# Cosine attention with a token and channel mixer: pair 0 loaded by heads, the end of batch 0 reordered, q and k loaded five pairs ahead

## The chip, the cores and the metric

The kernel runs on one core of a Trainium2 chip. The metric is the device time of one execution in microseconds (us); lower is better. Engines are named as the profile names them: PE is TensorE (matmuls), PEld its weight loads, DVE is VectorE, ACT is ScalarE, POOL is GpSimd, SP is SyncE, which issues most transfers. "Pair" means two heads of one batch; there are 8 batches of 6 pairs, so pairs 0 to 47. The kernel before takes 386.36 us (median of the first three runs).

## The reference, cut to what matters

```python
q_n = q / (norm(q) + 1e-6);  k_n = k / (norm(k) + 1e-6)      # (8, 12, 448, 64)
attn = softmax(q_n @ k_n.T / tau)                              # tau = 0.1
x = (attn @ v) as (8, 448, 768)
u = x + (relu(x.T @ w_tok1) @ w_tok2).T                        # token mixing, 448 -> 256 -> 448
out = u + relu(u @ w_ch1) @ w_ch2                              # channel mixing, 768 -> 1536 -> 768
```

## The kernel before

A pair goes through this: load q and k; square them (GpSimd or ScalarE); sum the squares (VectorE, `sums`); logarithm and exponential on ScalarE, then a small sum and a reciprocal on VectorE (`norms`); multiply by the reciprocal norm on GpSimd (`scale`); transpose (PE) and copy out (VectorE); score (PE) and exponential (ScalarE); output (PE) and division (VectorE); token mixing. Once the six pairs of a batch are through, channel matmuls of that batch fill PE. In the first batch there is none of that filler yet, so there every engine's order counts. In the orders in time of these traces POOL, VectorE and ScalarE do their instructions in the order in which they are recorded: POOL, for one, stands 0.96 us before the copy of w2n at 18.63 us, with pair 3's scale behind it. The source reads:

```python
def norms(i, a0=0, a1=2, dve=False):           # a: 0 is k, 1 is q
    ...
    if dve:
        nc.vector.tensor_reduce(out=rn, in_=ne, ...)
        nc.vector.reciprocal(out=rn, in_=rn)
        return
    nc.scalar.activation(out=rn, in_=st["ssq"][0:n, sl], func=AF.Ln, bias=tiny[0:n])
    nc.scalar.activation(out=ne[:, :, 0], in_=rn, func=AF.Exp, scale=0.5)

def scale(i, a, eng=None):
    eng = eng or nc.gpsimd
    ...
    eng.tensor_tensor(out=kq[...], in0=st["kq"][a][...], in1=_bcast_free(rn[...], E), op=ALU.mult)
# ... cut: square, sums, tpose, score, pv_wide, tok1, tok2, udma (a transposing DMA), m_ch1

with tc.manual_schedule():
    # ... cut: loads, pair 0's squares, norms and scales
    sums(1); norms(1)
    tpose(0, 1, 2); warm(3, True); tpose(0, 0, 1); warm(5, True)
    square(2, 0)
    weights_tok2()                             # POOL issues the load of w2n
    score(0, 0); score(0, 1)
    norms(1, dve=True)
    scale(1, 0); scale(1, 1, nc.vector)
    sums(2); norms(2)                          # pair 2's norms: between pair 0's scores
    cast_v(0)
    score(0, 2); warm(8); tpose(1); score(0, 3); warm(6)
    norms(2, dve=True)
    square(3, 1, act=True); square(3, 0)
    load_v(4); load_qk(6)

    for i in range(1, NPAIR):                  # NPAIR = 6
        if i == 1:
            scale(2, 0); scale(2, 1, nc.vector)     # q of pair 2 on VectorE
        else:
            scaled(i + 1)                           # k and q on GpSimd
            if i != 3:
                weights_ch1(max(i - 3, 0))          # 576 KB, issued by POOL
        load_qk(i + 6)
        score(i, 0); score(i, 1)
        sums(i + 2); norms(i + 2)
        if i >= 2:
            tok1(i - 2)
        pv_wide(i - 1)
        norms(i + 2, dve=True)
        cast_v(i); square(i + 3, 0)
        # ... cut
        if i == 1:
            place_w2()                              # POOL copies w2n into w2t
        # ... cut
    # ... cut: pair 6; then pair 7, where batch 0 ends:
        if i == NPAIR + 1:
            tok2(i - 2, pe=True); upose(i - 4, 2); upose(i - 2)
            sums(i + 2)
        pv_rest(i - 1); pv(i - 1, 0); pv(i - 1, 1)
```

## Time and profile before

| stretch (us) | what happens | what was full |
|---|---|---|
| 0 to 15 | loads, pair 0, no filler for PE | a chain over all engines |
| 15 to 38 | pairs 1 to 6, one per 4.18 us | ACT and POOL |
| 38 to 46 | the end of batch 0 | POOL; PE idle 1.26 of 7.54 us |
| 46 to 352 | pairs with channel matmuls between | PE |
| 352 to 385 | last channel matmuls | PE |

A row of the table by stretch gives the stretch, its length, then for each engine the busy time and in brackets the instructions, then the granted clock of PE (1.00 is full), the mean DMA share, and GB/s. The prediction below shows these rows. A row of the order in time gives the start, the duration, the engine, the source line, the operation and its tiles, and in square brackets how long the engine was idle before it and what ended that. First the table's row for the 14 us that follow batch 0, with its header:

```profile
core 0: us, PE busy (x) PEld busy (x) DVE busy (x) ACT busy (x) POOL busy (x), PEclk, DMA share, GB/s
46.00:60.00 14.00, 14.00 (x172) 8.84 (x173) 8.79 (x21) 11.34 (x19) 11.15 (x14) 1.00 1.17 240
```

PE doesn't idle there at all. And from ScalarE's order in time, its wait for the sums of pair 9's squares:

```profile
44.46 0.31 ACT L264 ACTIVATE rn<-ssq,tiny 112x16 f32<-112x16 f32 x1 [1.18 <-DVE ssq L253]
```

### The profile page before, as it was taken

To read this page: it belongs to the slowest core of one execution; us is meant where nothing else is said; L and a number is where in the kernel's file an instruction comes from. 1 tells how busy PE (TensorE), PEld (TensorE's weight loads), DVE (VectorE), ACT (ScalarE), POOL (GpSimd) and SP (SyncE) were. 2 spreads that over 40 slices of the span, in tenths; PEclk is the share of its full clock that TensorE was granted. 3 is DMA by queue.
4 is the path that set the end of the run, shared out by engine and by line. 5 is a ranking of instruction groups with operands and counts; after the bars stand their busy time and mean duration, and the time that the engine had idled before them with its cause. 6 is when DMAs were issued, how large, how long until landed. Compare 5 with 4: busy or idle time off the path is not lost.

```text
span 385.4 us, 10226 instructions
## 1 busy us (share of the span) xinstructions
PE 372.2 (97%) x4124; PEld 243.3 (63%) x4124; DVE 217.4 (56%) x520; ACT 226.6 (59%) x398; POOL 237.8 (62%) x383
## 2 busy tenths in 40 slices
PE   5989899999999999999999999999999999999995
PEld 4566566677656666667666666667666666665564
DVE  7789766777535674557545674566544674241032
ACT  5899687845665456855675466764675466601400
POOL 8799987979567667668557767768657733000000
PEclk9799999999999999999999999999999999999998
DMA  8999999995984888768894887977996745114023
GB/s 214 263 244 235 157 235 190 226 222 112 243 191 116 200 204 201 175 168 177 213 195 117 172 204 185 197 173 181 198 217 122 134 120 133 15 54 97 0 67 99
DMA packets 115423, 64.21 MB, mean 167 GB/s; under 512 B 71728, under 2 KB 111792, under 8 KB 115376
## 3 DMA queue, kind: packets, MB, share of 16 engines
q1 hardware_dynamic: 108944, 57.62, 68.2%
q0 software_dynamic: 5616, 5.21, 8.9%
q10 hardware_dynamic: 816, 0.73, 0.7%
q8 instruction: 32, 0.52, 0.6%
q14 instruction: 15, 0.12, 0.1%
HBM read 43.45 MB, written 11.01 MB: 141 GB/s over the span
## 4 chain that ended last, share of the span: by engine, by line
PE 87%; DMA 4%; ACT 4%; DVE 2%; POOL 1%; issue 1%; ACTq 0%; DVEq 0%; POOLq 0%
PE psF L449 28%; PE psG L433 28%; PE psO L362 9%; PE psS L323 7%; PE psU L407 5%; PE psR L393 5%; DMA ut<-u 3%; ACT pt L324 3%; PE psQ L330 2%; PE psO L345 1%; DMA qf<-in_q_dram 1%; PE pst L300 1%; ACT sq L235 1%; POOL sq L237 1%; DVE ssq L253 0%
## 5 line engine op out<-in xcount | busy, mean ns | idle before, releaser
L324 ACT ACTIVATE pt<-psS 128x896 f16<-128x896 f32 (+1 forms) x156 | 132.6, 916 | 58.2 <-PE psS L323 57.8
L433 PE MATMUL psG<-ut,wc1t 128*128 128x448 f16 x576 | 116.8, 352 | 0.5 <-DMA ut<-u 0.5
L449 PE MATMUL psF<-wc2t,gt 128*128 128x384 f16 (+2 forms) x684 | 116.2, 323 | 0.0
L436 ACT ACTIVATE gt<-psG 128x448 f16<-128x448 f32 x96 | 51.8, 540 | 63.0 <-PE psG L433 63.0
L276 POOL TENSOR_TENSOR kq<-kf,rn 128x384 f16<-128x384 f32 (+1 forms) x48 | 42.8, 892 | 73.6 <-DVE rn L262 70.3
L449 PEld LDWEIGHTS <-gt 128*128 128x128 f16 x684 | 64.2, 98 | 38.0
L433 PEld LDWEIGHTS <-wc1t 128*128 128x128 f16 x576 | 53.8, 98 | 44.9 <-issue 0.7
L453 DVE TENSOR_TENSOR ost<-psF,u 128x384 f32<-128x384 f32 (+2 forms) x65 | 34.5, 531 | 57.1 <-PE psF L449 56.9
L253 DVE TENSOR_REDUCE ssq<-sq 128x15 f32<-128x960 f32 (+2 forms) x49 | 55.8, 1140 | 4.2 <-ACT sq L235 3.6
L396 DVE TENSOR_SCALAR rt<-psR 128x256 f16<-128x256 f32 x48 | 20.1, 419 | 59.5 <-PE psR L393 59.4
L276 POOL TENSOR_TENSOR kq<-qf,rn 112x512 f16<-112x512 f32 x45 | 46.9, 1043 | 3.0
L323 PE MATMUL psS<-qk 64*128 64x448 f16 x312 | 41.7, 359 | 2.7 <-DVE qk L302 2.5
L237 POOL TENSOR_TENSOR sq<-kf 128x384 f32<-128x384 f32 (+1 forms) x46 | 40.1, 872 | 1.2 <-DMA kf<-in_k_dram 1.2
L362 PE MATMUL psO<-vt,pt 128*128 128x65 f16 (+1 forms) x1056 | 40.3, 193 | 0.2 <-DVE ut L424 0.2
L237 POOL TENSOR_TENSOR sq<-qf 112x512 f32<-112x512 f32 x39 | 40.5, 1039 | 0.0
L362 PEld LDWEIGHTS <-pt 128*128 128x128 f16 (+1 forms) x1056 | 35.2, 97 | 4.0 <-PE psS L323 1.0
L366 DVE TENSOR_TENSOR x<-psO,rec 128x256 f16<-128x256 f32 x84 | 35.6, 424 | 2.9
L410 DVE TENSOR_TENSOR u<-psU,x 128x512 f16<-128x512 f32 x48 | 32.3, 674 | 4.8 <-PE psU L407 3.6
L393 PEld LDWEIGHTS <-w1t 128*128 128x128 f16 x384 | 25.0, 98 | 9.0 <-issue 2.3
L407 PEld LDWEIGHTS <-w2t 128*128 128x128 f16 x384 | 24.9, 98 | 7.8 <-issue 1.5
L393 PE MATMUL psR<-x,w1t 128*128 128x128 f16 x384 | 29.3, 219 | 0.4 <-DVE u L410 0.3
L407 PE MATMUL psU<-rt,w2t 128*128 128x128 f16 x384 | 29.3, 219 | 0.2 <-DVE qk L302 0.2
(54 smaller groups left out, 282.8 us busy)
## 6 DMA issues: line engine op xcount, KB each, us to landing
qf<-in_q_dram SPq DMA_DIRECT2D x48, 224.0 KB, 4.2
kf<-in_k_dram SPq DMA_DIRECT2D x36, 192.0 KB, 3.4
vf<-in_v_dram SPq DMA_DIRECT2D x36, 192.0 KB, 3.7
vf<-in_v_dram SPq DMA_DIRECT2D x12, 224.0 KB, 7.3
out_dram<-ost SPq DMA_DIRECT2D x8, 336.0 KB, 3.6
wc1t<-in_moe_w_ch_dram POOLq DMA_DIRECT2D x4, 576.0 KB, 10.2
wc2t<-in_moe_w_ch_dram POOLq DMA_DIRECT2D x2, 1152.0 KB, 14.0
out_dram<-ost SPq DMA_DIRECT2D x8, 288.0 KB, 3.3
```

The costliest lines, as they stand in the source:

```text
L237: nc.gpsimd.tensor_mul(out=dst, in0=src, in1=src)
L253: nc.vector.tensor_reduce(out=st["ssq"][0:n, sl], in_=st["sq"][0:n, sl], axis=AXX.X, op=ALU.add)
L276: eng.tensor_tensor(out=kq[0:p, a, 0:n].rearrange("p c g e -> p g c e"), in0=st["kq"[a]][:].rearrange("p (g c) e -> p g c e", g=2), in1=_b ...
L323: nc.tensor.matmul(psS[:, hh, 0:S], qk[hb, c * n:c * n + 128], qm[hb], start=True, stop=True)
L324: nc.scalar.activation(out=pts[i % 2][0:n, 2 * S * c:2 * S * (c + 1)].rearrange("p (h s) -> p h s", h=2), in_=psS[0:n, :, 0:S], func=AF.Ex ...
L362: nc.tensor.matmul(psO[:, m, 0:E + 1], pts[i % 2][0:n, at:at + 128], vt[0:n, i % HP, nch * hh + c, 0:E + 1], start=(old(i) and c == 0), st ...
L366: nc.vector.tensor_tensor(out=st["x"][:, :, hh * E:(hh + 1) * E], in0=psO[:, :, 0:E], in1=_bcast_free(rec[:], E), op=ALU.mult)
L393: nc.tensor.matmul(psR[:, tt], w1t[:, w1[m], tt * 128:(tt + 1) * 128], st["x"][:, m], start=(m == 0), stop=(m == 3))
L407: nc.tensor.matmul(psU[:, m], w2t[:, tt, lo:lo + 128], st["rt"][:, tt], start=(tt == 0), stop=(tt == TT - 1))
L433: nc.tensor.matmul(psG[:, 0:S], wc1t[:, dt, ct * 128:(ct + 1) * 128], ut[b][:, dt].rearrange("p m s -> p (m s)")[:, lo:lo + S], start=(dt ...
L436: nc.scalar.activation(out=gt[:, ct, (b % 2) * S:(b % 2 + 1) * S], in_=psG[:, 0:S], func=AF.Relu)
L449: nc.tensor.matmul(psF[:, 0:hi - lo], gt[:, ct, at:at + 128], wc2t[:, ct, lo:hi], start=(ct == 0), stop=(ct == CT - 1))
```

## The change

It has three parts. **The prologue**: pair 0's q and k come in by heads on two queues, k of pair 0 is scaled and transposed in halves, and pair 1's norms and scales come earlier; to make room, pair 2's norms and both of its scales move behind pair 1's first exponential. **The end of batch 0**: PE's work is recorded in the order in which VectorE can serve it, and pair 6's output goes into a tile of two banks. **Loads**: from pair 3 on, q and k are loaded five pairs ahead instead of six.

```diff
+    def load_first(a, src):                      # q or k of pair 0, one head per queue
+        t = qkv.tile([SC, QS, E], FP32, ...)
+        for g, eng in ((0, nc.sync), (1, nc.scalar)):
+            eng.dma_start(out=t[:, NCH * g:NCH * (g + 1)]..., in_=src[0, g]...)
+        return t
-            (nc.scalar if nm == "k" and i < 3 else nc.sync).dma_start(
+            nc.sync.dma_start(
... cut: scale_part (scale of chunks c0 to c1), tpose with chunks, x_wide split from pv_wide
-        for dt in range(DT):
+        dts = (0, 1, 3, 4, 2, 5) if (b, ct) == (0, 0) else range(DT)
... prologue
-        scale(0, 0)
+        scale_part(0, 0, 0, 2, nc.gpsimd)
+        scale_part(0, 0, 2, NCH, nc.gpsimd)
...
-        sums(2)
-        norms(2)
         cast_v(0)
         score(0, 2)
...
-        norms(2, dve=True)
+        sums(2)
...
         for i in range(1, NPAIR):
-            if i == 1:
-                scale(2, 0)
-                scale(2, 1, nc.vector)
-            else:
+            if i > 1:
                 scaled(i + 1)
...
-            load_qk(i + 6)
+            if i != 3:
+                load_qk(i + (6 if i < 3 else 5))
             score(i, 0)
+            if i == 1:
+                norms(2)
+                norms(2, dve=True)
+                scaled(2)
             score(i, 1)
... the end of batch 0, at pair 7
             if i == NPAIR + 1:
+                upose(i - 4, 2)
                 tok2(i - 2, pe=True)
-                upose(i - 4, 2)
+                pv_wide(i - 1)
                 upose(i - 2)
+                x_wide(i - 1)
                 sums(i + 2)
-            pv_rest(i - 1)
-            pv(i - 1, 0)
-            pv(i - 1, 1)
+            else:
+                pv_rest(i - 1); pv(i - 1, 0); pv(i - 1, 1)
```

The same move of `load_qk` from six to five ahead is made for pair 6 and for all later pairs.

## The prediction

> **What bounds the kernel now.** I read first the page's busy shares, then a table of busy time by stretch, then the order of instructions in time for the first 46 us, and last the chain of work that ended last. The share of busy time alone says that TensorE (PE) is the bound; the table says where it isn't.
>
> ```profile
> PE 372.2 (97%) x4124; PEld 243.3 (63%) x4124; DVE 217.4 (56%) x520; ACT 226.6 (59%) x398; POOL 237.8 (62%) x383
> ...
> core 0: us, PE busy (x) PEld busy (x) DVE busy (x) ACT busy (x) POOL busy (x), PEclk, DMA share, GB/s
> ...
> 8.00:14.60 6.60, 5.49 (x41) 3.23 (x39) 5.06 (x11) 4.65 (x9) 5.39 (x7) 0.50 1.20 254
> 15.00:38.00 23.00, 20.29 (x360) 14.66 (x357) 19.81 (x42) 22.84 (x39) 22.04 (x25) 1.00 1.16 246
> 38.37:45.91 7.54, 6.28 (x90) 4.19 (x88) 6.49 (x16) 4.76 (x8) 7.54 (x9) 1.00 1.29 126
> 45.91:352.00 306.09, 305.75 (x3410) 199.97 (x3410) 173.68 (x423) 182.60 (x321) 195.40 (x319) 1.00 0.80 170
> ```
>
> From 45.91 to 352 us PE is busy 305.75 of 306.09 us, and the change leaves that work alone (as it does the last 33 us, a tail of matmuls). So only the first 46 us can pay. In them PE is not the bound: from 15 to 38 us ScalarE (ACT) is busy 22.84 of 23 us and GpSimd (POOL) 22.04, and the DMA engines carry about 250 GB/s throughout. Each pair of heads there takes 4.18 us (the first softmax exponential of pairs 1 to 6 starts at 15.38, 19.56, 23.74, 27.93, 32.11 and 36.30). From 8 to 14.6 us PE has half its clock (0.50). Between 38.37 and 45.91 no engine but POOL is full: that is the end of batch 0, a chain between PE and VectorE (DVE).
>
> ```profile
> 10.59 0.81 POOL L182 DMA_DIRECT2D w2n<-in_moe_w_tok_dram  x1 [0.64 <-DMA w1t<-in_moe_w_tok_dram]
> 11.41 1.06 POOL L276 TENSOR_TENSOR kq<-kf,rn 112x512 f16<-112x512 f32 x1
> ...
> 14.57 1.55 POOL L276 TENSOR_TENSOR kq<-kf,rn 112x512 f16<-112x512 f32 x1 [0.56 <-DVE rn L262]
> ...
> 18.63 0.99 POOL L185 COPY w2t<-w2n 128x896 f16<-128x896 f16 x1 [0.96 <-DMA w2n<-in_moe_w_tok_dram]
> 19.59 1.04 POOL L276 TENSOR_TENSOR kq<-kf,rn 112x512 f16<-112x512 f32 x1
> ...
> 32.01 13.02 DMA ut<-u
> 45.02 0.04 issue
> 45.07 0.92 PE psG L433 x4
> ```
>
> The first rows are POOL's own order: its first scale of pair 1's k stands behind an issue that waited for an earlier weight load, and from 18.63 us on POOL never stops until pair 7 is scaled at 38.23. The last three are the chain: the transposing DMA of pair 2's output, issued at 32.01, lands 13.02 us later, and the channel matmul that needs it starts then, at 45.07.
>
> **What the Trainium skill says.** "TensorE: Matmul & The Clock Gate", Part 1, says that the array runs at half clock after an idle window and gets the full one after about 3.4 us of sustained work. The trace agrees: PE did 0.82 us of work between 5 and 8 us, then had 0.50 until 14.6. "DMA: Bandwidth & Descriptors", Anatomy of one DMA, fits a DMA from GpSimd as 2.0 us plus bytes over 436 GB/s: 2.5 us for the 224 KB of w2n. The list of DMA issues has 8.0 us for it; with the engines saturated the formula doesn't hold, and I use 8.0. "VectorE: DVE Perf Modes", the TRN2 errata section, gives a float32 tensor_tensor as (N+151)/0.96 ns: 691 for 512 elements, 424 for 256. The trace has 691 and 425. So a product over both heads in one instruction costs 0.69 us where two cost 0.85; with the reciprocals (0.20 against 2 x 0.17) it saves 0.30 us of DVE.
>
> **The change part by part.**
>
> *Pair 0's load by heads.* q of pair 0 goes out in two halves on two queues, then k. Now q and k share the engines, and q lands at 4.27 us, k at 4.72. Their 448 KB move at some 270 to 350 GB/s, so q alone should land about 0.7 us sooner, k hardly. VectorE's norms of pair 0 end at 7.83 now; with k's square waiting for k I get 7.2. POOL is issuing the eight w1t loads until 7.42, so its scale of k starts at 7.45 rather than 7.92.
>
> *k in halves.* A scale of 1.04 us becomes two of about 0.55. The first half is transposed, copied out and scored while the second runs. First score at about 8.75 instead of 10.06. ACT, however, has pair 1's norms ahead of it in order, which need pair 1's squares summed (about 9.35 by my count), so the first exponential starts near 9.9 instead of 10.65: 0.7 us won.
>
> *What then waits.* The w2n issue still stands ahead of pair 1's k on POOL, and still needs w1t to have landed (10.3 us). So that scale starts at 11.1 to 11.4 as before, the fourth score of pair 0 follows it at about 13, and pair 1's first exponential comes at 13.9 to 15.0 against 15.38: 0.4 to 1.5 us won.
>
> *Pair 2.* Its norms move behind pair 1's first exponential, and both of its scales go to POOL (before, q was on DVE, 0.69 us). From that exponential: 0.86 for it, 0.53 for logarithm and exponential, 0.5 on DVE, then on POOL 2.04 (two scales), 0.6 (cast), 1.0 (square) and 1.0 (placing w2n): POOL reaches pair 3's scale 6.5 us after it, at 20.4 to 21.5 instead of 19.59. That is a loss of 0.8 to 1.9 us on POOL. Its 18.64 us of unbroken work for pairs 3 to 7 passes that on to pair 7. I choose 0.9. Unless w1t lands early, the prologue's gain is eaten here.
>
> *End of batch 0.* Between 38.37 and 45.91 PE has, at its pace in the chain: transposes 0.40, token matmuls 3 x 0.45 (one psR, two psU), pair 7's scores 0.67, transposes of outputs 0.60, pair 6's output 1.13, channel matmuls 1.14. Sum 5.29 of 7.54 us, so at most 2.25 us is waiting. The new order follows DVE: outputs of pair 4 are done before the transposes, the psO tile in the other pool takes no slot that DVE must free first, and pair 2's transposed block, late in landing, is used fifth of six instead of third (two matmuls, 0.38 us, of grace). Counted from POOL's end for pair 7: 1.25 us to the scores, then 0.67, 0.40, 0.65 (with a wait for rt), 1.13, 0.40 and 1.25, in all 5.75 us. With POOL 0.9 late, at 39.13, the first channel group ends at 44.9 against 45.98 now: 1.1 us won.
>
> *Loads five pairs ahead.* No bytes are saved. Pair 9's q and k (448 KB, about 1.8 us at 250 GB/s) no longer stand ahead of pair 2's transposing DMA, and pair 10's move behind it too, so it should land at 41.5 to 44, before its matmul needs it. The price: k of pairs 10 and 11 lands later (I get 45 and 52 where they landed at 39.0 and 49.8), and POOL already waited 1.2 us for k of pair 11. Some of this reaches PE through DVE's sums: I take 0.3 us of loss.
>
> Sum: 1.1 - 0.3 = 0.8 us by the count. A change of this kind to a tuned kernel is probably kept for a reason, and my count of POOL is the weakest part, so I choose 1.4 us.
>
> **The rivals.** (1) *POOL takes the place of ACT.* For it: the order above, and 22.04 busy of 23 us. At its worst, POOL 1.9 us late, it leaves 0.1 us of gain, and with loads late the kernel would be slightly slower, about 387. Against it: if w1t lands sooner because ACT's queue empties early, pair 1's scale starts a microsecond earlier, nothing is lost on POOL, and the gain is 2 us, with the clock regained earlier 2.5 to 3: about 383.5. (2) *The transposing DMA stays the wait.* It lands late where it runs beside the w1-channel weight load, and that load is still there. If it lands at 45.0 again, two matmuls follow instead of four: 0.4 us won, about 386. (3) *Late loads.* If POOL waits 3 us for pair 11 and the sums of that pair hold DVE, the gain goes in waits of PE between 50 and 60 us: about 386.3. (4) *Everything hidden:* 386.3, unchanged.
>
> **Range and chances.** Predicted 384.9 us. The two faster runs of before agree within 0.05 us (386.31 and 386.36; 392.23 is a slow one), so noise is small against 1 us. The good rival gives 383.5 or somewhat less, the bad one 387; eight times in ten 383.0 to 386.6. Two per cent is 7.7 us, far more than the 2.25 + 1.5 us that there is to win, and no part adds as much: 0.02 faster, 0.97 the same, 0.01 slower.
>
> **What would show it right or wrong.** First exponential at 9.9 us, pair 1's at 13.9 to 15.0; POOL at pair 3's scale at 20.4 to 21.5, and ACT with idle time between 18 and 38 us released by PE, which itself waits for POOL; the transposing DMA landing before 44 us; first channel group ending near 44.9; POOL waits for k between 44 and 54 us. From 60 us on PE as full as before. The prediction is wrong if POOL starts pair 3 no later than 19.6 (then the gain is larger), if PE idles over 0.5 us between 46 and 60 us (then it is smaller), or if later batches wait for q and k at all.

## The result, and the profile after

The changed kernel takes 388.92 us (median of four runs, 388.83 to 389.19) where the kernel before took 386.58 in the same rounds (386.31 to 392.23, the last a slow run). The ratio is 1.0064 (95 per cent interval 1.0044 to 1.0084): 2.3 us slower, inside two per cent. Ratios here are the mean time of one kernel's fast runs over that of the other's fast runs of the same rounds, so not quite the ratio of the medians. The output is correct, as in every run below.

One warning about the baseline. The profiled execution of before, with a span of 385.4 us, took 387.2 us (the span is 1.8 us shorter than the time), 0.6 above the median. Its milestones are those of a rather slow draw. I had read them as those of a typical run.

The page of the changed kernel, its span and its busy shares, and its table by stretch (columns as above):

```profile
span 386.8 us, 10208 instructions
...
PE 373.2 (96%) x4122; PEld 243.9 (63%) x4122; DVE 217.2 (56%) x520; ACT 226.8 (59%) x398; POOL 238.6 (62%) x385
```

```profile
8.00:14.60 6.60, 5.85 (x41) 2.87 (x41) 4.48 (x10) 4.84 (x8) 5.16 (x7) 0.60 1.19 260
15.00:38.00 23.00, 19.07 (x322) 13.78 (x320) 18.66 (x41) 21.43 (x38) 21.40 (x25) 0.97 1.17 228
38.37:45.91 7.54, 7.13 (x120) 5.16 (x116) 6.08 (x14) 5.64 (x9) 7.54 (x10) 1.00 1.09 209
46.00:60.00 14.00, 13.38 (x165) 8.32 (x164) 9.45 (x24) 10.83 (x21) 11.89 (x14) 1.00 1.14 234
60.00:352.00 292.00, 291.67 (x3242) 191.02 (x3240) 165.78 (x404) 171.94 (x303) 184.97 (x306) 1.00 0.77 166
```

The busy shares hardly differ. The table says where the difference is. From 60 us on PE is as full as before. From 15 to 38 us PE did 19.07 us of work, where it did 20.29 before: 1.22 less. ACT, which had been full there, lost 1.41 us. From 38.37 to 45.91 PE did 0.85 more (7.13 against 6.28): the end of batch 0 is tighter, as intended. From 46 to 60 it did 0.62 less. Of the sum, -1.22 + 0.85 - 0.62 = -0.99, most is the first term.

What happens in the first term is in POOL's order in time, from the issue of w2n to pair 3's first scale:

```profile
10.02 0.81 POOL L190 DMA_DIRECT2D w2n<-in_moe_w_tok_dram  x1
10.84 1.18 POOL L293 TENSOR_TENSOR kq<-kf,rn 112x512 f16<-112x512 f32 x1
...
12.54 1.03 POOL L245 TENSOR_TENSOR sq<-kf 112x512 f32<-112x512 f32 x1
16.60 1.04 POOL L293 TENSOR_TENSOR kq<-kf,rn 112x512 f16<-112x512 f32 x1 [3.03 <-DVE rn L270]
17.60 1.04 POOL L293 TENSOR_TENSOR kq<-qf,rn 112x512 f16<-112x512 f32 x1
...
20.14 1.01 POOL L193 COPY w2t<-w2n 128x896 f16<-128x896 f16 x1
21.09 1.06 POOL L293 TENSOR_TENSOR kq<-kf,rn 112x512 f16<-112x512 f32 x1
```

At 16.60 POOL has been idle for 3.03 us, waiting for `rn`, the reciprocal norms of pair 2, which now stand behind pair 1's first exponential (14.66 us) on ScalarE. Before, that scale of k started at 14.57 after a wait of 0.56. So it starts 2.03 us later. From there to pair 3's scale POOL takes 4.49 us where it took 5.02, though it now does both scales: it no longer waits 0.96 us for w2n, and its scale of k takes 1.04 instead of 1.55 us. The net is 2.03 - 0.53 = 1.50 us late (21.09 against 19.59). The rest of batch 0 inherits it: pair 7's first exponential starts at 42.15 instead of 40.76.

The end of batch 0 in the changed kernel, from the order in time of PE, VectorE and ScalarE:

```profile
44.66 1.30 PE L456 MATMUL psG<-ut,wc1t 128*128 128x448 f16 x6
45.43 0.69 DVE L406 TENSOR_TENSOR x<-psO,rec 128x512 f16<-128x512 f32 x1
46.04 1.21 DVE L261 TENSOR_REDUCE ssq<-sq 112x16 f32<-112x1024 f32 x1
47.28 0.31 ACT L272 ACTIVATE rn<-ssq,tiny 112x16 f32<-112x16 f32 x1 [2.61 <-DVE ssq L261]
48.88 1.04 PE L340 MATMUL psS<-qk 64*128 64x448 f16 x6 [0.55 <-DVE qk L319]
```

The first channel group ends at 45.95, at the time of before (45.98), with pair 7 1.39 us later: 1.4 us are recovered at this milestone. They are not recovered in the span: from pair 7's first exponential to the end it is about 344.65 us in both kernels (386.8 - 42.15 and 385.4 - 40.76). VectorE now does pair 9's sums (46.04) after the division of pair 6's output, ScalarE waits 2.61 us for them where it waited 1.18, and PE loses 0.55 us at 48.88 waiting for copies that VectorE made late. Five loads ahead did what it should: the transposing DMA of pair 2 lands at 41.08 instead of 45.02.

### The profile page after: what moved, and what is told of

The parts are those of the page before. It is cut to its first block, busy times and chain, and to the rows that moved or that the text cites. A ratio compares the mean times of both kernels' runs of the same rounds, so it can differ in the third digit from the quotient of the medians.

```text
span 386.8 us, 10208 instructions
## 1 busy us (share of the span) xinstructions
PE 373.2 (96%) x4122; PEld 243.9 (63%) x4122; DVE 217.2 (56%) x520; ACT 226.8 (59%) x398; POOL 238.6 (62%) x385
## 4 chain that ended last, share of the span: by engine, by line
PE 88%; POOL 3%; ACT 2%; DVE 2%; DMA 2%; issue 1%; SPq 1%; POOLq 0%; DVEq 0%
PE psF L472 28%; PE psG L456 28%; PE psO L379 9%; PE psS L340 8%; PE psU L429 5%; PE psR L415 5%; PE psQ L347 2%; DMA kf<-in_k_dram 2%; ACT pt L341 1%; POOL kq L293 1%; PE psO L362 1%; DVE ssq L261 1%; POOL sq L245 1%; PE pst L317 1%; PE psO L397 1%
## 5 line engine op out<-in xcount | busy, mean ns | idle before, releaser
L293 POOL TENSOR_TENSOR kq<-kf,rn 128x384 f16<-128x384 f32 (+1 forms) x47 | 41.4, 882 | 75.8 <-DVE rn L270 71.1
L293 POOL TENSOR_TENSOR kq<-qf,rn 112x512 f16<-112x512 f32 x46 | 48.0, 1044 | 3.0
L379 PE MATMUL psO<-vt,pt 128*128 128x65 f16 (+1 forms) x1024 | 39.2, 194 | 0.0
L383 DVE TENSOR_TENSOR x<-psO,rec 128x256 f16<-128x256 f32 x82 | 34.8, 424 | 2.8
L379 PEld LDWEIGHTS <-pt 128*128 128x128 f16 (+1 forms) x1024 | 34.2, 97 | 3.5 <-issue 0.9
```

The costliest lines, as they stand in the source:

```text
L293: eng.tensor_tensor(out=kq[0:p, a, 0:n].rearrange("p c g e -> p g c e"), in0=st["kq"[a]][:].rearrange("p (g c) e -> p g c e", g=2), in1=_b ...
L379: nc.tensor.matmul(psO[:, m, 0:E + 1], pts[i % 2][0:n, at:at + 128], vt[0:n, i % HP, nch * hh + c, 0:E + 1], start=(old(i) and c == 0), st ...
L383: nc.vector.tensor_tensor(out=st["x"][:, :, hh * E:(hh + 1) * E], in0=psO[:, :, 0:E], in1=_bcast_free(rec[:], E), op=ALU.mult)
```

## The experiments

Eighteen kernels ran, in five groups; those of a group ran on one chip and share the runs of before. All the results in one table. "Step" is the time from pair 1's first exponential to pair 2's; "pair 7" is the start of pair 7's first exponential; both, and the span, are of the one profiled execution, the median of all runs, the ratio of the fast runs.

| kernel | median us | before, same group | ratio (95%) | step 1 to 2 | pair 7 | span |
|---|---|---|---|---|---|---|
| before, first profile | 386.58 | | 1 | 4.18 | 40.76 | 385.4 |
| same_again (before) | 387.08 | 386.74 | 1.0008 (0.9990 to 1.0026) | 4.18 | 40.94 | 385.9 |
| after | 388.92 | 386.58 | 1.0064 (1.0044 to 1.0084) | 5.55 | 42.15 | 386.8 |
| pro_alone | 388.93 | 386.61 | 1.0052 (1.0024 to 1.0079) | 5.55 | 42.81 | 387.4 |
| end_alone | 386.87 | 386.61 | 0.9995 (0.9966 to 1.0025) | 4.19 | 40.59 | 384.7 |
| five_alone | 386.32 | 386.61 | 0.9987 (0.9960 to 1.0014) | 4.18 | 40.41 | 384.5 |
| pair2_back | 387.38 | 386.61 | 1.0021 (0.9988 to 1.0053) | 5.30 | 42.91 | 387.5 |
| sums9_early | 388.78 | 386.74 | 1.0053 (1.0039 to 1.0068) | 5.55 | 42.57 | 386.6 |
| w2_later | 387.27 | 386.74 | 1.0018 (1.0000 to 1.0036) | 4.18 | 40.30 | 386.5 |
| all_mended | 388.13 | 386.74 | 1.0037 (1.0007 to 1.0067) | 4.83 | 40.84 | 384.9 |
| six_mended | 387.65 | 387.01 | 1.0017 (0.9990 to 1.0044) | 4.19 | 40.34 | 384.6 |
| weights_later | 386.52 | 387.01 | 0.9994 (0.9975 to 1.0013) | 4.34 | 40.39 | 384.4 |
| six_weights_later | 387.50 | 387.01 | 1.0004 (0.9983 to 1.0025) | 5.57 | 42.27 | 386.2 |
| before_weights_later | 386.33 | 387.01 | 0.9982 (0.9965 to 0.9999) | 4.23 | 40.69 | 384.7 |
| k_act | 389.73 | 386.64 | 1.0068 (1.0042 to 1.0093) | 5.55 | 42.30 | 387.0 |
| k_act_pair2 | 387.53 | 386.64 | 1.0023 (0.9991 to 1.0055) | 4.32 | 40.55 | 385.3 |
| k_act_mended | 386.66 | 386.64 | 0.9996 (0.9970 to 1.0022) | 4.19 | 40.47 | 384.6 |
| old_loads | 389.31 | 387.30 | 1.0046 (1.0008 to 1.0084) | 5.55 | 42.99 | 387.2 |
| old_loads_pair2 | 387.39 | 387.30 | 0.9996 (0.9958 to 1.0033) | 4.19 | 40.95 | 385.2 |
| old_loads_mended | 386.37 | 387.30 | 0.9971 (0.9930 to 1.0012) | 4.19 | 40.92 | 384.5 |

A profile is of a single execution, and not always of a typical one: those of pair2_back (389.36 us), w2_later (388.39) and six_weights_later (388.04) are of their kernel's slowest run, that of all_mended (386.73) of one of its two fastest. All of these count as fast runs. The medians take in the slow ones: one of six_mended (392.61; its five fast runs have a median of 386.72) and one in each before but those at 386.61 and 387.01. The before at 387.30 also has a run of 391.6 that counts as fast.

### Which part costs it

The theory: the prologue's part loses on POOL what it gains, and the other two are level or gain. The rival: the reordered end of batch 0, with its new wait for sums, or the later loads, cost it. Each part was put alone into the kernel before.

**pro_alone**: before plus the prologue's part of the diff, nothing else.

> The kernel before with the prologue part alone. Theory A (the order on GpSimd): pair 2's norms behind pair 1's first exponential and both its scales on GpSimd make GpSimd reach pair 3's scale at about 21.1 us instead of 19.6, pair 7's first exponential comes about 1.4 us later than before (42.1 against 40.8), and the kernel is 1.0 to 1.5 us slower than before. Rival B (the loads five pairs ahead are what costs): this one is as fast as before or up to 0.7 us faster, since pair 0 starts 0.9 us sooner.

Measured: 388.93 us, 2.3 above before, the whole loss. POOL reaches pair 3's scale at 21.72, and pair 7 is at 42.81. The loss is larger than the 1.0 to 1.5 us expected.

**end_alone**: before plus the reordered end of batch 0.

> The kernel before with the new end of batch 0 alone. Theory: pair 7 starts on time (40.8 us), the first channel group ends 0.5 to 1.4 us sooner than 45.98 (held by the transposing DMA, which lands at about 45.0 as before), and then pair 9's sums of squares, which now stand behind pair 6's output on VectorE, hold ScalarE for 2 us or more and give about 0.9 us back: within 0.5 us of before. Rival: the new order is a plain gain and shows as 1 us or more.

Measured: 386.87 us, level (0.9995). The new wait of ScalarE for pair 9's sums is there without the rest of the change:

```profile
45.72 0.31 ACT L264 ACTIVATE rn<-ssq,tiny 112x16 f32<-112x16 f32 x1 [2.60 <-DVE ssq L253]
```

**five_alone**: before plus the loads five pairs ahead.

> The kernel before with q and k loaded five pairs ahead from the third pair on, nothing else. Theory A: the transposing DMA of pair 2 lands at 41 to 43 us instead of 45.0, the 0.47 us wait ahead of the third channel matmul goes, GpSimd waits under 1.5 us for k, and the kernel is 0 to 0.5 us faster than before. Rival B: late loads of k for pairs 10 and 11 hold GpSimd and with it the whole, and it is 1 us or more slower.

Measured: 386.32 us, level (0.9987). The transposing DMA of pair 2 lands at 38.71. It lands earlier and the time does not move: at that place the kernel waits for other things too.

What follows: the prologue's part is the loss. The second and third parts show no cost of their own within about 0.3 per cent, and no gain clear of the noise.

### Is it pair 2's place?

The theory: of the prologue's part it is the move of pair 2's norms and scales. The rival: it is the loading by heads, with later landings for k of pairs 1 and 2.

**pair2_back**: the changed kernel with pair 2 in its old place.

```diff
         scale(1, 0)
+        sums(2)
+        norms(2)
         cast_v(0)
 ...
-        sums(2)
+        norms(2, dve=True)
 ...
+            if i == 1:
+                scale(2, 0)
+                scale(2, 1, nc.vector)
 ...
-            if i == 1:
-                norms(2)
-                norms(2, dve=True)
-                scaled(2)
```

> The changed kernel with pair 2's sums, norms and scales where they stood before (norms between pair 0's second and third exponential, q scaled on VectorE). Theory A: GpSimd reaches pair 3's scale by 18.7 to 19.6 us instead of 21.1, pair 7's first exponential comes 1.4 to 1.9 us sooner than 42.15, and the kernel is 1.0 to 1.8 us faster than the changed one (about 387.4 or less on its scale of 388.9). Rival B: GpSimd's order is not what holds it, and it moves by less than 0.4 us.

Measured: 387.38 us, 1.5 less than the changed kernel, but with a spread of 2.8 us. The wait for norms is gone. In the profile, of the slowest run, POOL's order shows another wait in its place:

```profile
14.52 1.49 POOL L293 TENSOR_TENSOR kq<-kf,rn 112x512 f16<-112x512 f32 x1
...
20.87 1.00 POOL L193 COPY w2t<-w2n 128x896 f16<-128x896 f16 x1 [3.14 <-DMA w2n<-in_moe_w_tok_dram]
21.84 1.03 POOL L293 TENSOR_TENSOR kq<-kf,rn 112x512 f16<-112x512 f32 x1
```

Pair 2's k is scaled at 14.52 again, and then POOL stands 3.14 us before the copy of w2n, whose load hasn't landed. In before that wait was 0.96. So the late norms had hidden a late load. That this wait makes the spread is supported by the slowest run having it; no faster run of this kernel was profiled. The profile has a second delay, in PE's clock (see "What the runs settle"), so the spread is not shown to come from w2n alone.

**same_again**: the kernel before, unchanged, as a control.

> The kernel before, run as if it were an experiment: a ratio of 1.000 within 0.002, and a second profile of it. The first profile (span 385.4) was of a run that took 387.2 us, the runs since took 386.2 to 386.7; this one should have its first channel group end somewhat before 45.98 us, by up to 0.8.

Measured: ratio 1.0008. Its profile is of a run of 387.73 us and shows pair 7 at 40.94, the end at 385.9. Its first channel group ends at 46.52, where it was expected before 45.98. So milestones of two profiles of one program differ by 0.2 to 0.5 us, and the kernel before by itself ranges over more than a microsecond.

### The sums of pair 9, and the copy of w2n

**sums9_early**: the changed kernel with pair 9's sums ahead of the transposed outputs' copies on VectorE.

```diff
             if i == NPAIR + 1:
+                sums(i + 2)
                 upose(i - 4, 2)
 ...
                 x_wide(i - 1)
-                sums(i + 2)
```

> The changed kernel with pair 9's sums of squares on VectorE ahead of the transposed outputs instead of behind pair 6's output. Theory C (the new order at the end of batch 0 gives back what it wins because ScalarE's norms of pair 9 wait for those sums): ScalarE's wait of 2.61 us at 47.28 is gone, pair 8's first exponential comes 0.5 to 0.9 us sooner than 49.39 counted from the end of the first channel group, and the kernel is 0.4 to 0.9 us faster than the changed one (about 388.3). Rival: PE makes it up later or something else holds it there, and it moves by less than 0.3 us.

Measured: 388.78 us, 0.14 less than the changed kernel in other rounds: no difference. The wait is gone, as two lines of ScalarE's order show:

```profile
44.97 0.32 ACT L272 ACTIVATE rn<-ssq,tiny 112x16 f32<-112x16 f32 x1
...
46.78 0.54 ACT L459 ACTIVATE gt<-psG 128x448 f16<-128x448 f32 x1 [1.24 <-PE psG L456]
```

The logarithm runs at 44.97 without a wait, and PE is busy 14.00 of 14 us from 46 to 60. But the first channel group now ends 4.17 us after pair 7's first exponential (46.74 - 42.57), where it was 3.80 (45.95 - 42.15): the 1.2 us of sums delay VectorE's copies of the outputs. One wait was exchanged for another. From pair 7's first exponential to the end this profile takes 344.0 us (386.6 - 42.57) where the changed kernel's takes 344.65, but pair 7 came 0.42 us later in it, and in the times the mend pays at most a few tenths.

**w2_later**: pair2_back, with the copy of w2n behind pair 3's scales.

```diff
 scaled(i + 1)
+if i == 2:
+    place_w2()
 ...
-            if i == 1:
-                place_w2()
```

> Pair 2's norms and scales back where they stood, and besides the placing of the second token weight behind pair 3's scales on GpSimd. Theory A2 (what spreads the runs of the kernel with pair 2 back, 386.6 to 389.4, is the landing of that weight, at 20.8 us in the profiled one, for which GpSimd waits with pair 3's scales behind it): the spread shrinks to under 1 us, GpSimd reaches pair 3's scale by 19.0 us, and the median falls below 386.6. Rival: the spread has another cause and stays over 1.5 us.

Measured: 387.27 us, the spread down to 1.5 us; under 386.6 and under 1 us were expected. POOL reaches pair 3 at 17.70 and pair 7 comes at 40.30. Then the gain is lost again, as POOL's order shows:

```profile
17.70 1.04 POOL L293 TENSOR_TENSOR kq<-kf,rn 112x512 f16<-112x512 f32 x1 [0.78 <-DVE rn L270]
...
48.18 1.04 POOL L245 TENSOR_TENSOR sq<-kf 112x512 f32<-112x512 f32 x1 [4.38 <-DMA kf<-in_k_dram]
```

POOL, early now, waits 4.38 us for k of pair 10, one of the loads that the five-ahead rule made later: it was issued at 33.60 (30.08 in before) and took 14.4 us to land (8.9 in before). Only 3.5 of the 9 us are the later issue. Pair 8's first exponential follows pair 7's by 7.73 us, and pair 9's pair 8's by 8.29, where the changed kernel has 7.24 and 7.10. This profile is of the slowest run.

**all_mended**: w2_later with pair 9's sums early and the issue of w2n behind pair 1's scale.

```diff
-        weights_tok2()
         norms(1)
 ...
         scale(1, 0)
+        weights_tok2()
```

> The three mends together (pair 2 back, the weight placed later, pair 9's sums early) and pair 1's scale of k ahead of the issue of that weight on GpSimd. By the theories the prologue is 0.5 to 1 us ahead of before and the end of batch 0 another 1 us: 384.3 to 385.3, that is 1 to 2 us faster than the kernel before. If the mends don't add up it stays at 386 or above.

Measured: 388.13 us, with a spread of 3.9 us (386.72 to 390.6). The profile, of a fast run, has the milestones that I wanted (pair 7 at 40.84, span 384.9). The median doesn't: it lies 3 us above what was expected. I had the mechanism of the fast run and not that of the slow ones.

### Late loads: six ahead again, or the channel weights later

The theory: the mended kernels lose to late loads of k, so giving those loads an earlier place or a freer DMA removes it.

**six_mended**: pair2_back with w2n's copy later, pair 9's sums early and all loads six ahead again.

```diff
-                load_qk(i + (6 if i < 3 else 5))
+                load_qk(i + 6)
```

> The changed kernel with pair 2 back, the token weight placed later, pair 9's sums early, and q and k loaded six pairs ahead again. Theory D (with the prologue mended, what spreads the runs is k of pair 10 landing late because it is asked for late, as in the profile with a 4.38 us wait of GpSimd for it at 43.8 us): that wait is under 0.5 us, the transposing DMA lands at about 44 to 45 us again, and the time is 385.5 to 386.4 with a spread under 1.2 us. Rival: the spread comes from the clock or the weights, and stays at 2 us or more.

**weights_later**: the same with loads five ahead, and the channel weights issued later.

```diff
-                if i != 3:
-                    weights_ch1(max(i - 3, 0))
+                if i in (2, 4):
+                    weights_ch1(i // 2 - 1)
 ...
-        weights_ch1(3)
+        weights_ch1(2)
 ...
+            if i == NPAIR + 1:
+                weights_ch1(3)
```

> The changed kernel with pair 2 back, the token weight placed later, pair 9's sums early, loads five pairs ahead, and the third and fourth quarter of the first channel weight asked for one and two pairs later. Theory E (the weights' transfers, 576 KB each, share the engines with pair 2's transposing DMA and with k of pair 10 just when these are needed): k of pair 10 lands before 44.5 us in every run, the transposing DMA by 41, and the time is 384.6 to 385.6, faster than before by 0.8 to 1.8 us. Rival: the fourth quarter lands after 60 us and PE waits for it, 386.5 or more.

**six_weights_later**: both, six ahead and the weights later.

> The same with loads six pairs ahead. If the weights are the cause the depth of the loads matters little: within 0.5 us of the one with five. If the depth is the cause this one is 0.5 us or more faster than five.

**before_weights_later**: the kernel before with w2n's copy later and the channel weights later.

> The kernel before with only the token weight placed behind pair 3's scales and the two quarters of the channel weight later. By the theories GpSimd gets about 1 us of slack, the prologue stays bound by ScalarE at 4.18 us a pair, and the wait for the transposing DMA (45.0 us) shrinks: 385.6 to 386.2 us, 0.3 to 0.9 faster than before. Rival: nothing, within 0.2 us.

Measured, with before at 387.01: six_mended 387.65, weights_later 386.52, six_weights_later 387.50, before_weights_later 386.33. The theory is not borne out. six_mended stays outside its range even by its fast runs (386.72, over 2.3 us). In the profile of weights_later the loads landed as early as expected (k of pair 10 at 40.98), but the time did not follow. six_weights_later is 1.0 us slower than weights_later, where 0.5 us either way, or faster, was expected.

In that profile of weights_later the transposing DMA of pair 2 lands at 39.41, POOL reaches pair 3 at 17.63, and the span is 384.4. The profile of six_weights_later, of its slowest run, has the long step from pair 1 to pair 2 (5.57 us) without the late place of pair 2. k of pair 1 landed at 8.14, ACT waited 1.4 us and POOL 1.5 us for it, and pair 1's first exponential came at 15.53 (14.88 in weights_later). The long step after it goes with PE's clock, as read below; that a late load of k costs this step is not shown.

The transposing DMA takes 12.1 to 13.0 us in the profiles with loads six ahead, but 8.4 and 8.9 where the channel weights come later; with loads five ahead it takes 6.5 to 8.8, except 11.1 in k_act_pair2 and 13.1 in w2_later. And before_weights_later gets as far as weights_later without any of the prologue's change.

### Why k of pairs 1 and 2 lands later

In the profiles with pair 0's load by heads its q and k land at 3.3 to 3.6 and 4.2 to 4.5 us (4.3 to 4.5 and 4.6 to 5.0 before), but k of pair 1 at 6.8 to 8.1 (6.1 to 6.8 before) and k of pair 2 at 8.8 to 10.1 (7.7 to 8.6). First theory: the change also moved k of the first pairs from ScalarE's queue to SyncE's, behind each q. Rival: the split of pair 0's load itself.

**k_act**, **k_act_pair2**, **k_act_mended**: the changed kernel, pair2_back and weights_later, each with k of pairs 1 and 2 on ScalarE's queue again.

```diff
-            nc.sync.dma_start(
+            (nc.scalar if nm == "k" and i < 3 else nc.sync).dma_start(
 ...
+        load_qk(1)
+        load_qk(2)
         nc.scalar.add_instruction(mybir.InstLoadActFuncSet(
 ...
-        load_qk(1)
-        load_qk(2)
```

> The changed kernel with k of pairs 1 and 2 asked for on ScalarE's queue again (pair 0 still by heads). Theory F: they land by 6.8 and 8.7 us, GpSimd's square of pair 2 and ScalarE's square of pair 1 wait under 0.2 us, pair 1's first exponential moves from 14.7 to 14.2 or less, and the kernel is 0.4 to 0.9 us faster than the changed one: 388.0 to 388.5. Rival: the order on GpSimd alone decides and it is within 0.2 us of 388.9.

> The same with pair 2's norms and scales where they stood. If these two are the whole loss: 386.0 to 386.6, level with before or up to 0.5 us faster, with a spread no larger than that of before (1.8 us). Rival: still 387 or above, the rest is elsewhere.

> The best mended version (pair 2 back, the token weight placed later, pair 9's sums early, channel weights later) with k of pairs 1 and 2 on ScalarE's queue: 385.3 to 386.0, under before (386.5) in every round, spread under 1.2 us. Rival: 386.5 as without it.

Measured: k of pair 1 lands at 7.4 to 7.5 us and k of pair 2 at 9.2 to 9.3. That is not the time of before, so the theory of the queue falls. This agrees with the Trainium skill, "DMA: Bandwidth & Descriptors", Issuing engines are not separate DMA queues, which says that transfers run on the same 16 engines and interleave whichever engine issued them. The three times are 389.73, 387.53 and 386.66. The first two differ in pair 2's place alone, on the same chip and in the same rounds, and by 2.2 us. POOL's order of k_act, and after it that of k_act_pair2:

```profile
16.73 1.04 POOL L293 TENSOR_TENSOR kq<-kf,rn 112x512 f16<-112x512 f32 x1 [2.74 <-DVE rn L270]
...
21.23 1.06 POOL L293 TENSOR_TENSOR kq<-kf,rn 112x512 f16<-112x512 f32 x1
```

```profile
13.83 1.55 POOL L293 TENSOR_TENSOR kq<-kf,rn 112x512 f16<-112x512 f32 x1
...
18.52 1.00 POOL L193 COPY w2t<-w2n 128x896 f16<-128x896 f16 x1 [1.59 <-DMA w2n<-in_moe_w_tok_dram]
19.47 1.06 POOL L293 TENSOR_TENSOR kq<-kf,rn 112x512 f16<-112x512 f32 x1
```

With the old place pair 2 is scaled 2.90 us sooner and pair 3 1.76 us sooner, in spite of a wait of 1.59 us for w2n.

**old_loads**, **old_loads_pair2**, **old_loads_mended**: these three with pair 0's load in one piece too.

```diff
-        half[0] = {}
-        pipe[0] = {"q": load_first("q", q), "k": load_first("k", k)}
+        load_qk(0)
```

> The changed kernel with pair 0 to 2 loaded as before (whole pairs, q and k on two queues). Theory G (loading by heads opens a hole of about 0.8 us in the transfers that later loads pay for): k of pair 1 lands by 6.8 us and of pair 2 by 8.7; pair 0's first exponential comes 0.2 to 0.6 us later than 9.8, pair 1's no later than 14.66; with pair 2's norms still late the kernel is 0 to 0.6 us faster than the changed one (388.3 to 388.9). Rival: loading by heads is a gain, and it is 0.5 us or more slower than the changed one.

> The same with pair 2's norms and scales where they stood. If these two are the whole loss: 386.0 to 386.8, level with before. Rival: 387.3 or more.

> The best mended version with pairs 0 to 2 loaded as before: 385.5 to 386.2, faster than before (386.5) by 0.3 to 1 us, and spread under 1.2 us. Rival: as weights_later, 386.5.

Measured: k of pairs 1 and 2 lands where it did before, so the split of pair 0's load is what moves it. The times are 389.31, 387.39 and 386.37, with before at 387.30. The first two again differ in pair 2's place alone: 1.9 us. Loading in one piece didn't make the changed kernel faster (ratio 1.0046 against 1.0064, intervals overlapping): the first exponential is back at 10.53 and k of pair 1 arrives in time, but in its profile pair 7 comes at 42.99 against 42.15. POOL's order of old_loads_pair2 (the DMA that the first line names had landed at 8.21, so that short wait is put down wrongly):

```profile
14.48 1.55 POOL L293 TENSOR_TENSOR kq<-kf,rn 112x512 f16<-112x512 f32 x1 [0.16 <-DMA kf<-in_k_dram]
...
18.18 0.98 POOL L193 COPY w2t<-w2n 128x896 f16<-128x896 f16 x1 [0.60 <-DMA w2n<-in_moe_w_tok_dram]
19.11 1.05 POOL L293 TENSOR_TENSOR kq<-kf,rn 112x512 f16<-112x512 f32 x1
```

Its wait for w2n is 0.60 us, the shortest of the three kernels with pair 2 in its old place and the copy at its old place.

Why the split slows the loads behind it is open. Every profile with it moves less from 3.4 to 4.8 us than any without it: 128 to 252 GB/s on the average of these 1.4 us, against 282 to 336. The lines give GB/s from 2 to 10 us in slices of 0.2 us, first for the kernel before, then for the changed one:

```profile
GB/s 148 56 164 251 374 379 394 354 343 297 225 266 287 292 287 256 261 261 225 210 287 277 287 256 323 246 256 241 261 287 271 246 208 216 284 269 264 246 241 271
```

```profile
GB/s 36 189 348 384 384 359 364 138 143 169 159 159 92 128 220 292 353 374 364 343 274 241 312 271 248 271 243 297 269 254 243 284 264 251 223 225 279 269 279 213
```

From 3.4 to 4.8 us the changed kernel moves 92 to 169 GB/s where before moves 225 to 354. No run here tells what the engines did in that time.

### What the runs settle

The five kernels with pair 2 behind pair 1's exponential (after, pro_alone, sums9_early, k_act, old_loads) all have a step of 5.55 us from pair 1 to pair 2 and a time 2.0 to 3.1 us above their before. The others have 4.18 to 4.34, but for three: all_mended 4.83, pair2_back 5.30 and six_weights_later 5.57. The three pairs of kernels that differ in this place alone give -1.5 (after and pair2_back, in different groups), -2.2 and -1.9 us. **That the late place of pair 2's sums, norms and scales costs 1.5 to 2.2 us is shown.** Which part of it, the later sums and norms or q's scale moving from VectorE to GpSimd, was not separated. Of each difference 0.2 to 0.3 us lies outside the profiled span: the time less the span is about 2.1 us in each run of after, k_act and old_loads, and 1.8 to 1.9 in each run of their partners. The reason is open.

**PE's clock, a rival that no run tested, can be read in the traces.** PE has half its clock in the prologue of every profile and gets the full one back at about 13.4 to 15.1 us with the old prologue, and at 14.5 to 18.5 us with the new one. (The clock column reads 1.00 from the start in end_alone, five_alone and pair2_back. Their warm-up matmuls, 107 ns apart at first and 56 ns later as in the other profiles, show the half clock.) In the five kernels with the late place the clock is not the cause: it comes back between 15.6 us (old_loads) and 17.9 us (sums9_early), and the step is 5.55 us in all. In the others the long steps go with it: back by 15.4 us, the step is 4.18 to 4.34; at 16.3 us (all_mended), 4.83; at 17.5 (pair2_back), 5.30; at 18.5 (six_weights_later), 5.57. In pair2_back PE's output of pair 0 takes 1.94 us, and ACT then waits 1.00 us for PE's scores. In weights_later, where the full clock is back at 15.2, the output takes 1.29 us (last line):

```profile
15.27 1.94 PE L397 MATMUL psO<-vt,pt 112*128 112x65 f16 x32
18.32 1.73 ACT L341 ACTIVATE pt<-psS 112x896 f16<-112x896 f32 x2 [1.00 <-PE psS L340]
```

```profile
14.90 1.29 PE L397 MATMUL psO<-vt,pt 112*128 112x65 f16 x32
```

What this costs in the time was not measured: the profile of all_mended is of a fast run. So the spread of the kernels with pair 2 put back has at least two candidates, late loads and the clock, and its cause stays open. Of the twelve kernels from w2_later on, eleven came out 0.1 to 2.8 us above the range expected of them.

No version clearly beats the kernel before. The best, old_loads_mended at 386.37 and before_weights_later at 386.33, have ratios of 0.9971 (0.9930 to 1.0012) and 0.9982 (0.9965 to 0.9999). That is 0.2 to 0.3 per cent; the first ratio owes half of it to the run of 391.6 in its before, and the second interval only just clears 1.

## Why the prediction was right or wrong

**Direction and size: wrong.** It said 384.9, and 383.0 to 386.6 as the range; it is 388.92. "Within 2 per cent" held.

**The bound, and where time could move: right.** From 60 us on PE is as full as before; everything happens in the first 60 us.

**First exponentials: right in the trace, wrong in worth.** Pair 0's starts at 9.79 (predicted 9.9), pair 1's at 14.66 (predicted 13.9 to 15.0). But the four later profiles of kernels with the old prologue (same_again, end_alone, five_alone, before_weights_later) have pair 1's at 14.99 to 15.25, not 15.38. And with pair 2 put back, what is left of the new prologue reaches pair 7 at 40.30 to 40.95, the two slowest runs named above aside; the old prologue reaches it at 40.41 to 40.94. With loads by heads and pair 2 in its old place, pair 1's first exponential comes at 14.85 to 15.16, the slowest run (15.53) aside, so most of the 0.9 us won at pair 0 is gone one pair later, and nothing of it can be seen at pair 7.

**POOL at pair 3: the mechanism right, the term mis-sized.** This is the first step that failed. The prediction gave a loss of 0.8 to 1.9 us and said "I choose 0.9". It measured 1.50 in the trace, and as time 1.5 to 2.2 in the three pairs of kernels. The sum behind it was right: from pair 1's first exponential to pair 3's scale POOL takes 6.43 us (21.09 - 14.66), predicted 6.5. The choice of 0.9 put that exponential near 14.0, at the favourable end of its range. The first rival, POOL in the place of ACT, is what happened. Its worst case was put at 387, with "0.1 us of gain" left at POOL 1.9 us late, and that was too mild, because the gains set against it were not there. ACT's idle time between 18 and 38 us, named as the sign, shows as 21.43 busy against 22.84.

**A term missed on both sides.** The scale of k on GpSimd took 1.55 us in before and 1.04 in the changed kernel. In before VectorE's scale of q (14.53 to 15.22) ran beside it. The Trainium skill, "GPSIMD Engine Reference", section 1, Specifications, states that GpSimd's path to SBUF is shared with VectorE and contended by VectorE instructions with two SBUF inputs. The trace agrees: 0.51 us more with 0.65 us of overlap. This made the loss smaller, not larger.

**End of batch 0: the milestone moved, the gain did not come.** This is the second step that failed: 1.1 us were booked as time won because the first channel group would end that much sooner. It ends at 45.95, not 44.9. Of the 1.05 us, 0.6 is POOL later than chosen (it ends pair 7's scales at 39.74, not 39.13) and 0.45 the chain, 6.2 us long and not 5.75. Relative to pair 7, 1.4 us are recovered, but what is done sooner for the group is done later for the rest. After the group's end 339.41 to 339.94 us follow in the five profiles with the old order, 340.05 to 341.22 in the eight with the new order as it stands, and 339.48 to 340.05 in the seven with the new order and pair 9's sums early. So the group's end was no measure of the whole. Nor was there as much waiting as the prediction counted: it took 7.54 - 5.29 = 2.25 us for the most that could be waiting, but its own row has PE busy 6.28 us, which leaves 1.26. The wait for pair 9's sums, which the new order makes, was not in the prediction. PE idles 0.62 us from 46 to 60 us, over the 0.5 that was named as a sign of a smaller gain. The prediction's 0.3 us of loss was booked there too, but for late loads. When end_alone was run on its own, the time did not move.

**Loads five ahead: right on the DMA, its cost elsewhere.** The DMA landed at 41.08 (predicted 41.5 to 44). The waits for k between 44 and 54 us did not come in the changed kernel, because POOL is late there itself: it waits for k 0.8 us in all, where it waited 1.2. They came in w2_later (4.38 us), where POOL is early, and there the DMA landed at 44.73 with loads five ahead too.

**The added 0.6 us: baseless.** "A change of this kind to a tuned kernel is probably kept for a reason" turned a count of 0.8 into 1.4. No view stood behind it. Without it the prediction would have been 385.5, still with the wrong sign.

**The baseline: not typical.** Its milestones came from a run 0.6 us slower than the median, so part of the waiting that the change was to remove is less in most runs. The loss adds up this way: pair 7 is 1.4 us later than in that profile, that profile was itself 0.6 above the median, and the rest, some 0.3 us, lies outside the profiled span: the time less the span is 2.1 us in all four runs of the changed kernel and 1.7 to 1.8 in every run of before. end_alone has 2.1 as well, pro_alone 1.8; the reason is open.

**The clock: one draw.** The prediction read half the clock until 14.6 us from one profile of before (0.5 us slices give 14.8). In the second profile of the same program, same_again, the half clock runs only from about 9.9 to 13.4 us.

## What to carry to other kernels

When work is moved behind another engine's instruction to start something sooner, follow the moved work to the first engine that has no slack, and book its delay there in full. Don't take one milestone, such as the end of the first group of matmuls, for the whole: ask what was put behind it. An earlier start ahead of a steady pace is worth only what is still there several steps later. Take the milestones of the baseline from more than one profiled run when the hoped gain is near the spread of the runs. Compare the granted clock of two profiles before a longer step is put down to anything else. And settle which part of a change costs by pairs of kernels that differ in one place only: here three such pairs agreed where single profiles, each of one run, did not.

## What the Trainium skill lacked or had wrong

- "DMA: Bandwidth & Descriptors", Anatomy of one DMA: its fit gives an estimate of 2.5 us for the 224 KB of w2n. With the engines saturated (DMA share 1.16 to 1.20) it took 8.0 us in before, and 7.3 to 10.1 us over the profiles. The page's fit has no term for load on the engines.
- The same page, Rules for kernel authors, says of the DMA transpose that beside ordinary DMAs it "needs nothing". That is about correctness, and no result here was wrong. It doesn't tell that such a transpose can be slow: pair 2's, beside a weight load issued by GpSimd, took 13.0 us in before and 7.6 in the changed kernel. In before the engines moved 24 to 61 GB/s for some 3 us around it, as this line shows (GB/s from 30 to 46 us in slices of 0.4 us, the kernel before):

```profile
GB/s 236 328 320 341 298 287 90 156 279 246 225 200 257 218 250 287 200 234 286 333 277 92 45 42 45 28 24 46 61 82 82 134 159 129 143 219 241 279 277 279
```

- No page has it that the first load of a program, split by heads over two queues, lets the loads behind it land about 1 us later (k of pair 1 at 7.5 us on the average of the twelve profiles with it, 6.5 on that of the eight without), with 128 to 252 GB/s moved between 3.4 and 4.8 us, against 282 to 336.
